# An attention and gated-MLP kernel in fp32r: operands of its matmuls at another distance modulo 256 bytes

## The chip, the cores and the metric

The kernel runs on one core of one Trainium2 chip. The metric is the device time of the program in microseconds. Before the change it is 687.74 us in the median of three runs (687.03 to 688.06). The engines are named as in the profile: PE is TensorE's matmul, PEld its weight load, DVE VectorE, ACT ScalarE, POOL GpSimd, and SPq the queue from which SyncE issues transfers. A matmul has a stationary operand, which a weight load puts into the array, and a moving operand, which streams through it.

## The reference

All inputs are fp32. There are 8 batches, 12 heads, 448 positions, a head dimension of 64, a model width of 768 and a hidden width of 1024 (two halves of 512).

```python
# attention with a sigmoid in place of the softmax
scores = scale * np.matmul(q, k.transpose(0, 1, 3, 2)) - np.log(S)
attn = 1.0 / (1.0 + np.exp(-scores))
x = np.matmul(attn, v)                     # heads side by side: (8, 448, 768)
# gated MLP with a spatial product
h = np.maximum(x @ w_in, 0.0)
u, v = h[..., :512], h[..., 512:]
v_n = (v - mean(v)) / np.sqrt(var(v) + 1e-6)
v_s = np.einsum('ts,bsd->btd', w_spatial, v_n) + b_spatial[None, :, None]
out = (u * v_s) @ w_out
```

## The kernel before

Most products are made in the number type fp32r, to which an fp32 value is split as a high and a low part: a cast gives the high part, a subtraction the low one. A product of two split operands is three matmuls, in the order of `TERMS` (line 224): high times high, low stationary times high moving, high stationary times low moving. Each matmul loads its stationary operand of 128 columns anew. Tiles of split operands hold both parts one behind the other in the same partition.

The work goes over four pairs of batches (`m`). Within a pair these stages follow on TensorE, and the names are those of the profile:

- Scores `psc` (line 249): for a pair of heads that lies in the two halves of the partitions, 128 keys are stationary and 448 queries moving. Two matmuls of 64 rows each run beside each other, one per head. Keys and queries lie in one tile, `qks`: 384 keys at its start, the queries from column `REST` = 384 on. The last 64 keys of two heads are multiplied in plain fp32 from the loaded tile `raw` (line 237).
- `pav` (line 279): attention times values in plain fp32; stationary the values `v`, moving the sigmoids `at`. Its result is split into `x_s`, which holds 12 heads of two batches.
- `pv` (line 290, as all below): the v half of the hidden layer, 128 positions of `x_s` stationary, 512 columns of `w_in` moving.
- `pg`: the spatial product, normalised values `vn` stationary, `w_sp_s` moving with 448 columns.
- `pu`: the u half, `w_in` stationary and `x_s` moving with 448 columns.
- `po`: the output, `w_out_s` stationary and the gated values `gs` moving with 448 columns.

The order is written out by hand: `attention`, the loop at the end of the program, and `in_program_order`, which keeps each engine to the order in which the program names its work. Transfers are all issued from SyncE's queue, several heads ahead (`start_loads`, `ahead`). VectorE and ScalarE split the loaded keys and queries (`attention_splits`), empty the accumulators and split the results.

SBUF positions follow from the pools. The pool `small` comes first; an unused tile `fill` of 152 columns stands at its end (line 95). Then come the constants in the order of lines 97 to 101, then the buffers of `work`, each kind (`raw`, `v`, `tmp`, `big`, `split`, `wval`) with as many buffers as it asks for. In the built program of before, each of these tiles starts in its partition at a multiple of 256 bytes, and so does each slice of them that a matmul reads.

Of the kernel before, what the change touches and what calls it, by code (L numbers as in the profile page):

```python
# [8 lines left out]
F32 = mybir.dt.float32  # L9
F32R = mybir.dt.float32r  # L10
# [4 lines left out]
P = 128  # L15
# [20 lines left out]
def attn_gmlp_kernel(  # L36
# [25 lines left out]
    nc = tc.nc  # L62
    B, NHP, _, _ = qk.shape
    S = out.shape[3]
    D = P // 2
    NCC = out.shape[1]
    DM = NCC * P
    F = w_in.shape[1] // (4 * NCC)
    NFC = F // P
    HALF = 64  # L70
    NFULL = 3

    REST = NFULL * P
    PART = REST + S
    QK = 1.0 / math.sqrt(D)
    NEG_LOG_S = -math.log(S)
# [2 lines left out]
    small = ctx.enter_context(tc.tile_pool(name="small", bufs=2))  # L79
    const = ctx.enter_context(tc.tile_pool(name="const", bufs=1))  # L80
    work = ctx.enter_context(tc.tile_pool(name="work", bufs=2))
# [10 lines left out]
    table = small.tile([P, 1], F32, name="table", bufs=1)  # L92
    nc.scalar.activation(table, bias_s, AF.Sigmoid)

    small.tile([P, 152], F32, name="fill", bufs=1)

    w_in_s = const.tile([P, 2 * NCC, 2, F], F32R, name="w_in_s")
    w_out_s = const.tile([P, NFC * DM // 512, 2, 512], F32R, name="w_out_s")
    w_sp_s = const.tile([P, 4, 2, 512], F32R, name="w_sp_s")
    b_bc = const.tile([P, 512], F32, name="b_bc")  # L100
    x_s = const.tile([P, 2, NCC, 2 * S], F32R, name="x_s")

    def split(hi, lo, src, copy):
        copy(hi, src)  # L104
        nc.vector.tensor_sub(lo, src, hi.bitcast(F32))  # L105
# [30 lines left out]
    def weight_steps():  # L136

        steps = []
        for i in range(NCC):
            steps += [(w_in, w_in_s, NCC + i)] + [(w_sp, w_sp_s, i)] * (i < NFC)  # L140
        steps += [(w_in, w_in_s, i) for i in range(NCC)]
        steps += [(w_out, w_out_s, i) for i in range(NFC * DM // 512)]
        raws = {}

        def load(n):
            if n < len(steps):
                src, _, i = steps[n]
                w = 512 if src is w_sp else 1024

                if n < NFIRST:  # L150
                    raw = work.tile([P, 1024], U32, tag="tmp", name=f"wraw_{n}", bufs=3)[:, :w]
                else:
                    raw = work.tile([P, 1024], U32, tag="raw", name=f"wraw_{n}", bufs=4)
                raws[n] = raw.bitcast(F32) if src is w_sp else raw
                nc.sync.dma_start(raws[n], src[:, i * w : (i + 1) * w])

        for n in range(AHEAD):
            load(n)
        yield
        for n, (src, dst, i) in enumerate(steps):  # L160
            load(n + AHEAD)
            if src is w_sp and i == 0:
                nc.sync.dma_start(b_bc, b_sp.broadcast_to([P, 512]))
            hi, lo = dst[:, i, 0], dst[:, i, 1]
            val = raws.pop(n)
            if src is not w_sp:
                raw = val
                val = work.tile([P, 512], U32, tag="wval", name=f"wval_{n}", bufs=1)
                yield from convert(val, raw)
                val = val.bitcast(F32)  # L170
            split(hi, lo, val, nc.vector.tensor_copy)
            yield


    NFIRST = NCC + NFC + 3
    BLOCK = 3

    weights = weight_steps()

    def load_weights(n):  # L180
# [4 lines left out]
    values = {}  # L185

    def attention_loads(b, hp):
        raw = work.tile([P, 1024], F32, tag="raw", name=f"raw_{b}_{hp}", bufs=4)[:, : 2 * S]
        cut = REST - P if b == hp == 0 else 0
        nc.sync.dma_start(raw[:, cut:], qk[b, hp, :, cut:])  # L190
        if cut:
            nc.sync.dma_start(raw[:, :cut], qk[b, hp, :, :cut])
        loaded[b, hp] = raw
# [13 lines left out]

    def attention_splits(b, hp):
        raw = loaded[b, hp]
        s = work.tile([P, 2, PART], F32R, tag="split", name=f"qks_{b}_{hp}", bufs=3)  # L210
        if b == hp == 0:

            chunk, rest, query = slice(REST - P, REST), slice(0, REST - P), slice(REST, PART)
            nc.vector.tensor_copy(s[:, 0, chunk], raw[:, chunk])
            for cols in (query, rest):
                nc.scalar.copy(s[:, 0, cols], raw[:, cols])
            for cols in (chunk, query, rest):
                nc.vector.tensor_sub(s[:, 1, cols], raw[:, cols], s[:, 0, cols].bitcast(F32))
        else:
            scalar = b == 1 or b == 0 and hp not in (1, 2)  # L220
            split(s[:, 0], s[:, 1], raw[:, :PART], nc.scalar.copy if scalar else nc.vector.tensor_copy)
        parts_of[b, hp] = s

    TERMS = ((0, 0), (1, 0), (0, 1))
# [4 lines left out]
    def attention_scores(b, hp, t):  # L229
# [3 lines left out]
        if t == NFULL:  # L233
            for odd in range(2):
                raw = loaded[b, hp + odd]
                for j, rows in enumerate(heads):
                    nc.tensor.matmul(  # L237
                        psc[odd * HALF : (odd + 1) * HALF, j, :S],
                        raw[rows, PART : PART + HALF],
                        raw[rows, REST:PART],  # L240
                        start=True,
                        stop=True,
                    )
        else:
            s = parts_of[b, hp + t // (NFULL + 1)]
            k = (t % (NFULL + 1) + NFULL - 1) % NFULL * P
            for i, (a, e) in enumerate(TERMS):
                for j, rows in enumerate(heads):
                    nc.tensor.matmul(  # L249
                        psc[:, j, :S],  # L250
                        s[rows, a, k : k + P],
                        s[rows, e, REST:PART],
                        start=i == 0,
# [40 lines left out]
    def gate_values(m, ts):  # L294

        n = len(ts)
        pv = banks(f"pv_{m}_{ts[0]}")
        for i, t in enumerate(ts):
            product(
                pv[:, i, :F],  # L300
                [
                    (
                        lambda a, cc=cc, t=t: x_s[:, a, cc, t * P : (t + 1) * P],
                        lambda c, cc=cc: w_in_s[:, NCC + cc, c, :],
                    )
                    for cc in range(NCC)
                ],
            )
        rv = work.tile([P, 2, 512], F32, tag="tmp", name=f"rv_{m}_{ts[0]}", bufs=3)
        nc.scalar.activation(rv[:, :n], pv[:, :n], AF.Relu)  # L310
        mv = small.tile([P, 2, 2], F32, tag="mv", name=f"mv_{m}_{ts[0]}")
        for i in range(n):
            stats = small.tile([P, 6], F32, tag="stats", name=f"stats_{m}_{ts[i]}")
            nc.vector.bn_stats(stats, rv[:, i])  # L314
            nc.vector.bn_aggr(mv[:, i], stats)
        rstd = small.tile([P, 2], F32, tag="rstd", name=f"rstd_{m}_{ts[0]}")
        nc.gpsimd.tensor_scalar_add(rstd[:, :n], mv[:, :n, 1], 1e-6)
        nc.gpsimd.tensor_tensor(rstd[:, :n], rstd[:, :n], mhalf[:, :n], op=ALU.pow)
        for i in range(n):
            nc.vector.tensor_scalar_sub(rv[:, i], rv[:, i], mv[:, i, 0:1])  # L320
        for i, t in enumerate(ts):
            vn = work.tile([P, 2, 512], F32R, tag="big", name=f"vn_{m}_{t}", bufs=7)
            if t != NFULL:
                parts = [(vn[:, 0], vn[:, 1], slice(0, P))]
            else:

                a, c = slice(0, HALF), slice(HALF, P)
                parts = [(vn[a, 0], vn[c, 0], a), (vn[c, 1], vn[a, 1], c)]
            for hi, lo, rows in parts:
                nc.vector.tensor_scalar_mul(hi, rv[rows, i], rstd[rows, i : i + 1])  # L330
                nc.vector.scalar_tensor_tensor(
                    lo,
                    rv[rows, i],
                    rstd[rows, i : i + 1],
                    hi.bitcast(F32),
                    op0=ALU.mult,
                    op1=ALU.subtract,
                )
            vns[t] = vn
# [33 lines left out]
    def gated(b, fcs):  # L373

        odd = b % 2
        g = gates.pop((b, fcs))
        pu = banks(f"pu_{b}_{fcs[0]}")
        for i, fc in enumerate(fcs):
            fs = slice(fc * P, (fc + 1) * P)
            product(  # L380
                pu[:, i, :S],
                [
                    (
                        lambda a, cc=cc: w_in_s[:, cc, a, fs],
                        lambda c, cc=cc: x_s[:, c, cc, odd * S : (odd + 1) * S],
                    )
                    for cc in range(NCC)
                ],
            )
        nc.vector.scalar_tensor_tensor(g, pu[:, :, :S], 0.0, g, op0=ALU.max, op1=ALU.mult)  # L390
        products[b, fcs] = g
# [13 lines left out]
    def output(b, es, part=None):  # L405
# [9 lines left out]
        po = sums_of[es]  # L415
        n = NFC // 2
        for i, e in enumerate(es):

            def weight(a, fc, e=e):
# [6 lines left out]
                    (lambda a, fc=fc: weight(a, fc), lambda c, fc=fc: hidden[b, fc][:, c])  # L426
                    for fc in (range(NFC) if part is None else range(part * n, (part + 1) * n))
                ],
# [70 lines left out]
    load_weights(1)  # L499

    zeros = work.tile([P, 512], F32R, tag="big", name="zeros", bufs=7)
    nc.vector.memset(zeros.bitcast(F32), 0.0)  # L502
    idle = banks("idle")
    for _ in range(6):
# [98 lines left out]
```

## Time and profile before

| what | value |
|---|---|
| median of three runs | 687.74 us (687.03 to 688.06) |
| the profiled execution | 687.04 us |
| its span, first to last instruction | 685.3 us |
| matmuls and weight loads | 3838 each |
| mean granted clock of TensorE | 0.999 |

The span is the time from the first to the last instruction of one execution that the hardware profiler recorded; 1.7 us of that execution lie outside it. A row of a group gives its line, engine, operation, result and operands, shapes and count, then the busy time in us and the mean duration of one in ns, then the idle time of its engine before it and what ended that. A row of the chain gives its start and length in us, the engine, the result, the line and the count. A row of a tile's view gives the count, the least, median and greatest duration in ns, and the first and last start in us.

Plain fp32 matmuls appear in the trace as two instructions each. Matmuls overlap, since a matmul's record ends when its last result is out, and the next stream begins earlier.

### The profile page before, as it was taken

The numbers are of one execution on the slowest core, as the hardware profiler recorded it, in microseconds if no ns is written. First come the engines' busy times: TensorE is split into PE (matmuls) and PEld (weight loads), VectorE is DVE, ScalarE is ACT, GpSimd is POOL, SyncE is SP. The second block draws the span as 40 slices with busy tenths as digits, with TensorE's granted clock in tenths as the row PEclk, the third lists the DMA queues.
The fourth block names the chain that finished last, engine by engine and source line by source line (L and its number), as shares of the span: only waits on it lengthen the run. The fifth ranks groups of instructions, "written<-read, shape, count | busy, mean of one in ns | idle before, by whom it ended". The sixth has DMA issues, their size and how long they took to land.

```text
span 685.3 us, 9090 instructions
## 1 busy us (share of the span) xinstructions
PE 679.9 (99%) x3838; PEld 504.2 (74%) x3838; DVE 293.6 (43%) x471; ACT 240.9 (35%) x285; POOL 18.5 (3%) x36
## 2 busy tenths in 40 slices
PE   9999999999999999999999999999999999999997
PEld 5454889998554488999854458899984455889997
DVE  6999888803244237221233514721224241562111
ACT  7886110112577510011367651011137774101111
POOL 0000010000000001000000001100000000110000
PEclk9999999999999999999999999999999999999999
DMA  8872202230534000003062400000315310000102
GB/s 324 299 258 85 87 5 85 88 129 27 174 123 162 28 1 0 1 28 107 28 205 96 158 28 0 1 1 27 108 55 188 120 43 1 0 1 0 55 28 80
DMA packets 20552, 55.37 MB, mean 81 GB/s; under 512 B 1952, under 2 KB 8352, under 8 KB 20512
## 3 DMA queue, kind: packets, MB, share of 16 engines
q1 hardware_dynamic: 20512, 54.80, 23.4%
q8 instruction: 30, 0.49, 0.3%
q14 instruction: 10, 0.08, 0.0%
HBM read 43.78 MB, written 11.01 MB: 80 GB/s over the span
## 4 chain that ended last, share of the span: by engine, by line
PE 99%; DVE 0%; issue 0%; ACT 0%; ACTq 0%
PE pav L279 20%; PE po L290 17%; PE pu L290 17%; PE pv L290 17%; PE psc L249 15%; PE pg L290 10%; PE psc L237 3%; PE idle L505 0%; ACT osb L437 0%; DVE zeros L502 0%; DVE bias_s L88 0%; DVE mhalf L90 0%; ACTq L437 0%
## 5 line engine op out<-in xcount | busy, mean ns | idle before, releaser
L257 ACT ACTIVATE at<-psc,bias_s 128x896 f32<-128x896 f32 x168 | 158.5, 1008 | 60.0 <-PE psc L249 57.6
L279 PE MATMUL pav<-at,v 128*64 128x448 f32 (+1 forms) x768 | 139.4, 546 | 0.0
L290 PE MATMUL po<-gs,w_out_s 128*128 128x448 f32 x576 | 118.6, 366 | 0.0
L290 PE MATMUL pu<-x_s,w_in_s 128*128 128x448 f32 x576 | 118.0, 365 | 0.0
L290 PE MATMUL pv<-w_in_s,x_s 128*128 128x512 f32 x504 | 115.4, 390 | 0.0
L290 PEld LDWEIGHTS po<-gs,w_out_s 128*128 128x128 f32 x576 | 107.9, 188 | 9.7 <-ACT at L257 0.9
L290 PEld LDWEIGHTS pu<-x_s,w_in_s 128*128 128x128 f32 x576 | 108.2, 188 | 8.6
L290 PEld LDWEIGHTS pv<-w_in_s,x_s 128*128 128x128 f32 x504 | 94.3, 188 | 22.3 <-issue 2.8
L249 PEld LDWEIGHTS psc<-qks 64*128 64x128 f32 x864 | 76.8, 185 | 39.3 <-ACT at L257 15.5
L279 PEld LDWEIGHTS pav<-at,v 128*64 128x64 f32 (+1 forms) x768 | 44.0, 135 | 82.2 <-issue 76.5
L249 PE MATMUL psc<-qks 64*128 64x448 f32 x864 | 102.6, 377 | 0.2
L105 DVE TENSOR_TENSOR x_s<-pav,x_s 128x448 fp32r<-128x448 f32 x48 | 29.6, 623 | 125.6 <-ACT x_s L104 125.6
L290 PE MATMUL pg<-w_sp_s,vn 128*128 128x448 f32 x352 | 72.7, 365 | 0.0
L290 PEld LDWEIGHTS pg<-w_sp_s,vn 128*128 128x128 f32 x352 | 66.1, 188 | 5.4
L390 DVE SCALAR_TENSOR_TENSOR g<-pu,g 128x896 f32<-128x896 f32 x16 | 17.4, 1090 | 121.3 <-PE pu L290 121.3
L441 ACT COPY osb<-po 128x896 f32<-128x896 f32 x23 | 20.9, 907 | 118.4 <-PE po L290 110.2
L104 ACT CAST gs<-g 128x896 fp32r<-128x896 f32 x16 | 15.1, 941 | 129.9 <-DVE g L390 129.9
L310 ACT ACTIVATE rv<-pv 128x1024 f32<-128x1024 f32 (+1 forms) x16 | 14.8, 922 | 100.8 <-PE pv L290 100.8
L105 DVE TENSOR_TENSOR qks<-raw,qks 128x832 fp32r<-128x832 f32 x47 | 48.2, 1025 | 1.8 <-ACT qks L104 0.5
L104 DVE CAST qks<-raw 128x832 fp32r<-128x832 f32 x38 | 22.3, 586 | 32.6 <-PE po L290 31.1
L104 ACT CAST x_s<-pav 128x448 fp32r<-128x448 f32 x48 | 25.5, 532 | 28.7 <-PE pav L279 28.7
L314 DVE BATCH_NORM_STATS2 stats<-rv 128x6 f32<-128x512 f32 x28 | 19.0, 679 | 38.5 <-ACT rv L310 38.5
(38 smaller groups left out, 229.8 us busy)
## 6 DMA issues: line engine op xcount, KB each, us to landing
raw<-qk_dram SPq DMA_DIRECT2D x47, 448.0 KB, 4.3
v<-v_dram SPq DMA_DIRECT2D x23, 448.0 KB, 4.5
out_dram<-osb SPq DMA_DIRECT2D x23, 448.0 KB, 2.6
wraw<-w_in_dram SPq DMA_DIRECT2D x12, 512.0 KB, 4.1
wraw<-w_out_dram SPq DMA_DIRECT2D x6, 512.0 KB, 3.7
wraw<-w_sp_dram SPq DMA_DIRECT2D x4, 256.0 KB, 5.3
out_dram<-osb SPq DMA_DIRECT2D x2, 224.0 KB, 2.1
raw<-qk_dram SPq DMA_DIRECT2D x1, 320.0 KB, 2.9
```

The source lines that it names most:

```text
L104: copy(hi, src)
L105: nc.vector.tensor_sub(lo, src, hi.bitcast(F32))
L237: nc.tensor.matmul(psc[odd * HALF : (odd + 1) * HALF, j, :S], raw[rows, PART : PART + HALF], raw[rows, REST:PART], start=True, stop=True,)
L249: nc.tensor.matmul(psc[:, j, :S], s[rows, a, k : k + P], s[rows, e, REST:PART], start=i == 0, stop=i == len(TERMS) - 1,)
L257: nc.scalar.activation(at, psc[:, :, :S], AF.Sigmoid, bias=bias_s, scale=QK)
L279: nc.tensor.matmul(pav[heads, :S], vt[rows, t, heads], at[rows, j], start=start, stop=stop)
L290: nc.tensor.matmul(ps, st, mv, start=start and i == 0, stop=stop and i == len(ops) - 1)
L310: nc.scalar.activation(rv[:, :n], pv[:, :n], AF.Relu)
L314: nc.vector.bn_stats(stats, rv[:, i])
L390: nc.vector.scalar_tensor_tensor(g, pu[:, :, :S], 0.0, g, op0=ALU.max, op1=ALU.mult)
L441: nc.scalar.copy(osb, whole_of.pop(es)[:, :, :S])
```

## The change

The change moves tiles in SBUF and leaves what is computed as it is. It has four parts:

- `w_in_s` becomes two tiles, `w_v_s` and `w_u_s`. The tensor `w_in` is cut into the same two halves, and the list of loads names them in the same order as before.
- The constants are declared in another order: `w_sp_s`, `x_s`, `w_v_s`, an unused tile `fill_u` of 192 bytes, `w_u_s`, `w_out_s`, `b_bc`. The tile `fill` shrinks from 152 to 24 columns. An unused tile `fill_split` of 64 bytes is put into `work` ahead of `split`.
- Keys and queries lie 16 columns (64 bytes) further apart: `REST` is 400 where it was 384. The host puts 16 zeros between them, each head pair's load has 912 columns where it had 896, and its split 848 where it had 832.
- The buffers for `qks` are declared with the 896 columns per part that `gs`, which shares them, had already.

In the built program this gives the following positions, in bytes modulo 256; before, all are 0.

| matmuls | count | stationary after | moving after | stationary minus moving after |
|---|---|---|---|---|
| `psc`, line 249 (keys, queries) | 864 | 0 | 64 | 192 |
| `pg` (`vn`, `w_sp_s`) | 352 | 192 | 0 | 192 |
| `pu` (`w_u_s`, `x_s`) | 576 | 192 | 0 | 192 |
| `po` (`w_out_s`, `gs`) | 576 | 192 | 0 | 192 |
| `pv` (`x_s`, `w_v_s`) | 504 | 0 | 0 | 0 |
| `pav` (`v`, `at`) | 768 | 192 | 192 | 0 |
| `psc`, line 237 (short keys, queries in `raw`) | 192 | 0 | 0 | 0 |

```diff
+    w_u, w_v = (w_in[:, j * 2 * NCC * F : (j + 1) * 2 * NCC * F] for j in range(2))
...
-    REST = NFULL * P
+    FULL = NFULL * P
+    GAP = 16
+    REST = FULL + GAP
     PART = REST + S
...
-    small.tile([P, 152], F32, name="fill", bufs=1)
-
-    w_in_s = const.tile([P, 2 * NCC, 2, F], F32R, name="w_in_s")
+    small.tile([P, 24], F32, name="fill", bufs=1)
+
+    w_sp_s = const.tile([P, 4, 2, 512], F32R, name="w_sp_s")
+    x_s = const.tile([P, 2, NCC, 2 * S], F32R, name="x_s")
+    w_v_s = const.tile([P, NCC, 2, F], F32R, name="w_v_s")
+    const.tile([P, 48], F32, name="fill_u")
+    w_u_s = const.tile([P, NCC, 2, F], F32R, name="w_u_s")
     w_out_s = const.tile([P, NFC * DM // 512, 2, 512], F32R, name="w_out_s")
-    w_sp_s = const.tile([P, 4, 2, 512], F32R, name="w_sp_s")
     b_bc = const.tile([P, 512], F32, name="b_bc")
-    x_s = const.tile([P, 2, NCC, 2 * S], F32R, name="x_s")
...
-        raw = work.tile([P, 1024], F32, tag="raw", name=f"raw_{b}_{hp}", bufs=4)[:, : 2 * S]
-        cut = REST - P if b == hp == 0 else 0
+        raw = work.tile([P, 1024], F32, tag="raw", name=f"raw_{b}_{hp}", bufs=4)[:, : 2 * S + GAP]
+        cut = FULL - P if b == hp == 0 else 0
...
-        s = work.tile([P, 2, PART], F32R, tag="split", name=f"qks_{b}_{hp}", bufs=3)
+        s = work.tile([P, 2, 2 * S], F32R, tag="split", name=f"qks_{b}_{hp}", bufs=3)
...
-            split(s[:, 0], s[:, 1], raw[:, :PART], nc.scalar.copy if scalar else nc.vector.tensor_copy)
+            split(s[:, 0, :PART], s[:, 1, :PART], raw[:, :PART], nc.scalar.copy if scalar else nc.vector.tensor_copy)
...
-                        lambda c, cc=cc: w_in_s[:, NCC + cc, c, :],
+                        lambda c, cc=cc: w_v_s[:, cc, c, :],
...
-                        lambda a, cc=cc: w_in_s[:, cc, a, fs],
+                        lambda a, cc=cc: w_u_s[:, cc, a, fs],
...
     zeros = work.tile([P, 512], F32R, tag="big", name="zeros", bufs=7)
+    work.tile([P, 16], F32, tag="fill_split", name="fill_split", bufs=1)
...
-    qk = np.concatenate([full[:, :, P:], full[:, :, :P], q, short], axis=2)
+    gap = np.zeros((B, H, 16, D), q.dtype)
+    qk = np.concatenate([full[:, :, P:], full[:, :, :P], gap, q, short], axis=2)
```

More of the change, by code (lines that the diff above doesn't have):

```diff
@@ L139, in weight_steps @@
         for i in range(NCC):
-            steps += [(w_in, w_in_s, NCC + i)] + [(w_sp, w_sp_s, i)] * (i < NFC)
-        steps += [(w_in, w_in_s, i) for i in range(NCC)]
+            steps += [(w_v, w_v_s, i)] + [(w_sp, w_sp_s, i)] * (i < NFC)
+        steps += [(w_u, w_u_s, i) for i in range(NCC)]
         steps += [(w_out, w_out_s, i) for i in range(NFC * DM // 512)]
@@ L209, in attention_splits @@
         raw = loaded[b, hp]
-        s = work.tile([P, 2, PART], F32R, tag="split", name=f"qks_{b}_{hp}", bufs=3)
+        s = work.tile([P, 2, 2 * S], F32R, tag="split", name=f"qks_{b}_{hp}", bufs=3)
         if b == hp == 0:
-            chunk, rest, query = slice(REST - P, REST), slice(0, REST - P), slice(REST, PART)
+            chunk, rest, query = slice(FULL - P, FULL), slice(0, FULL - P), slice(REST, PART)
             nc.vector.tensor_copy(s[:, 0, chunk], raw[:, chunk])
@@ L568 @@
     full, short = k[:, :, :H0], k[:, :, H0:]
-    qk = np.concatenate([full[:, :, P:], full[:, :, :P], q, short], axis=2)
-    qk = np.ascontiguousarray(np.transpose(qk, (0, 1, 3, 2))).reshape(B, H // 2, 2 * D, 2 * S)
+    gap = np.zeros((B, H, 16, D), q.dtype)
+    qk = np.concatenate([full[:, :, P:], full[:, :, :P], gap, q, short], axis=2)
+    qk = np.ascontiguousarray(np.transpose(qk, (0, 1, 3, 2))).reshape(B, H // 2, 2 * D, 2 * S + 16)
     vT = np.transpose(v.reshape(B, H // 4, 2, 2, S, D), (0, 1, 4, 2, 3, 5)).reshape(B, H // 4, S, 2, 2 * D)
```

## The prediction

> **What bounds the kernel now.** I read the page first: the engines' shares, the granted clock, and the chain that ended last.
>
> ```profile
> span 685.3 us, 9090 instructions
> ...
> PE 679.9 (99%) x3838; PEld 504.2 (74%) x3838; DVE 293.6 (43%) x471; ACT 240.9 (35%) x285; POOL 18.5 (3%) x36
> ...
> PEclk9999999999999999999999999999999999999999
> ...
> PE 99%; DVE 0%; issue 0%; ACT 0%; ACTq 0%
> PE pav L279 20%; PE po L290 17%; PE pu L290 17%; PE pv L290 17%; PE psc L249 15%; PE pg L290 10%; PE psc L237 3%; PE idle L505 0%; ACT osb L437 0%; DVE zeros L502 0%; DVE bias_s L88 0%; DVE mhalf L90 0%; ACTq L437 0%
> ```
>
> TensorE is busy for 99% of the span, the chain is TensorE for 99%, and the clock is granted in full throughout. So no wait can be taken away; what moves the time is how far apart the matmuls start. The busy rows by group don't tell that, since matmuls overlap: one `pu` lasts 365 ns, but the next begins long before. The pieces of the chain do tell it, because a piece of n matmuls in a row that takes t has a spacing of t/n.
>
> ```profile
> 68.81 28.78 PE pv L290 x126
> 97.59 8.92 PE pg L290 x44
> 106.51 14.59 PE pu L290 x72
> ...
> 130.02 14.59 PE po L290 x72
> ...
> 188.39 2.04 PE psc L249 x18
> ```
>
> `pu`, `po` and `pg` all stream 448 columns: 14.59/72 = 202.6 ns, 202.6 ns and 8.92/44 = 202.7 ns apart. `pv` streams 512 columns: 28.78/126 = 228.4 ns. The scores `psc` run in pairs, one head in each half of the rows, so 18 of them are nine pairs, 227 ns a pair with the entry after another kind of matmul counted in.
>
> Per column the 512-wide product takes 228.4/512 = 0.446 ns and the 448-wide one 202.6/448 = 0.452 ns. At `pv`'s rate 448 columns would take 199.9 ns. So each 448-wide product has 2.7 ns that the wider one has not, although a cost fixed per product would weigh on both alike in ns. The spread of the durations points to the same place:
>
> ```profile
> L290 PEld LDWEIGHTS pu<-x_s,w_in_s x576: 187/188/188, 106.1 to 666.6; 128*128 128x128 f32 x192
> L290 PE MATMUL pu<-x_s,w_in_s x576: 362/365/369, 106.3 to 666.8; 128*128 128x448 f32 x192
> ...
> L290 PE MATMUL pv<-w_in_s,x_s x504: 389/389/499, 68.7 to 605.1; 128*128 128x512 f32 x168
> ...
> L290 PE MATMUL pg<-w_sp_s,vn x352: 362/365/370, 97.4 to 637.6; 128*128 128x448 f32 x176
> ...
> L249 PEld LDWEIGHTS psc<-qks x864: 182/184/334, 4.4 to 570.4; 64*128 64x128 f32 x173
> L249 PE MATMUL psc<-qks x864: 355/362/739, 4.4 to 570.6; 64*128 64x448 f32 x173
> ```
>
> The three numbers are the least, the median and the greatest duration. `pv` lies at 389 from its least to its median, while `pu` and `pg`, whose work is the same every time, go from 362 to 369 or 370. The weight load of 187 to 188 ns is the same in all. Something makes the 448-wide streams uneven by a few ns, with a weight load running beside each of them (PEld is busy 74% of the span). A clash of two reads, of the next stationary operand and of the stream under way, is one thing that could do this, and the distance of their addresses is what the change alters.
>
> **The change part by part.** The order of instructions on all five engines stays the same, one for one; no instruction is added or removed.
>
> *Addresses.* Before, every operand of a matmul starts at a multiple of 256 bytes. After, the stationary operand is 192 past the moving one, modulo 256, in `pu` (576), `po` (576), `pg` (352) and the scores of line 249 (864 matmuls, 432 pairs): 1936 places in the row of TensorE. In `pv`, `pav` and the 64-key scores the difference stays 0. The trace of before holds no matmul with another difference than 0, so the price is bounded from both sides. At the favourable end, the next weight load starts only when a product starts, so a spacing can't fall below the load of 188 ns: 202.6 - 188 = 14.6 ns less, times 1936 = 28.3 us. At the other end stands the worst duration that these streams now show, 370 against 365: 5 ns more, 9.7 us. I see no reason that excludes either sign. Between them I take the row that is nearest in kind: the same engine, load and number type, without the unevenness, `pv`. That is 2.7 ns less per place, and the least durations (362 against 365, 3 ns) say about the same. So 1504 x 2.7 = 4.1 us from `pu`, `po` and `pg`, and 432 x 2.7 = 1.2 us from the scores; of these the scores are the less certain, since their entries hide the steady spacing.
>
> *A rule against it.* The Trainium skill, "TensorE: Matmul & The Clock Gate" (Step-by-step, LDWEIGHTS), says that TensorE reads SBUF through two independent ports, so that loading the next weights takes no bandwidth from the running matmul. By that rule this term is nothing and the time stays; it is the first rival below. The same page's formula for spacing, N/2.4 + 2.5 ns, would give 189.2 ns for 448 columns against the 202.6 measured, so the page leaves 13 ns of each product unexplained, and a sum by it, were they all to go, would be about 26 us.
>
> *The gap between keys and queries.* It widens 47 splits from 832 to 848 columns, and the loads by the same 16 columns.
>
> ```profile
> L105 DVE TENSOR_TENSOR qks<-raw,qks 128x832 fp32r<-128x832 f32 x47 | 48.2, 1025 | 1.8 <-ACT qks L104 0.5
> L104 DVE CAST qks<-raw 128x832 fp32r<-128x832 f32 x38 | 22.3, 586 | 32.6 <-PE po L290 31.1
> ...
> raw<-qk_dram SPq DMA_DIRECT2D x47, 448.0 KB, 4.3
> ```
>
> 16/832 of the two VectorE rows (48.2 and 22.3 us) is 1.4 us, and ScalarE's nine casts of 885 ns add 0.2 us. The cover is TensorE's own stream: VectorE is idle for 57% of the span. In the first stage, where VectorE is busiest, the cover is thinnest; if all of that were exposed, it would cost 1.6 us. A load grows from 448 to 456 KB, 1.8% of 4.3 us or 0.08 us, and it is issued far ahead, except the first, which TensorE awaits: 656 columns instead of 640, some 0.07 us of its 2.9 us. I take 0.1 us for the whole.
>
> ```profile
> L104 ACT CAST qks<-raw 128x832 fp32r<-128x832 f32 x9 | 8.0, 885 | 0.0
> ...
> raw<-qk_dram SPq DMA_DIRECT2D x1, 320.0 KB, 2.9
> ```
>
> *`w_in` in two tiles, the order of the tiles, the fills.* The same loads into the same number of bytes, no instruction: 0. No other work hides this; there is nothing to hide.
>
> Sum: -4.1 - 1.2 + 0.1 = -5.2 us. The profiled execution took 687.04 us with a span of 685.3, so 1.7 us lie around the span and don't change: 687.04 - 5.2 = 681.8. The median of the three runs, 687.74, is 0.7 above the profiled one; on its level the forecast is 682.5 us.
>
> **The rivals.**
>
> *Nothing happens.* The two reads don't meet, and the uneven beat comes from elsewhere (the accumulation, the issue). For it: the load's duration is the same 187 to 188 ns beside 448 and 512 columns, as if nothing disturbed it, and `pu`, `po` and `pg` have one spacing although their operands lie in different tiles. Against it: a beat in work that never varies wants a cause, and two streams that run beside each other are at hand. The time would be 687.04 + 0.1 on the profiled level, 687.8 on the median's. This is also what the skill's rule above gives.
>
> *It opens the whole gap.* If nearly all that a 448-wide product takes above its weight load is a clash, which 192 bytes avoid, the spacing falls towards 188 ns: 14.6 x 1936 = 28 us, 659 us; half of it, 673 us. For it: nothing on the page accounts for the distance from 188 to 202.6. Against it: `pv` with its smooth beat pays per column almost the same, which suggests that most of this is the stream itself.
>
> *The new distance clashes more.* The stationary read is slower per byte than the stream: 128 columns in 188 ns against 448 in 202.6. So the stream runs through the addresses modulo 256 several times while one load runs, and overtakes it at some moment whatever the distance; 192 bytes choose only the moment. If it falls where the stream has just settled, each product takes the place of today's worst, 369 or 370 against 365: 4 ns more on 1936 places, 7.7 us, 695.5 us on the median's level. It decides as soon as the spacing of `pu` exceeds 203.4 ns (0.7 ns x 1936 = 1.4 us). For it: today's common distance 0 lets some products through at 362, so it is not the worst. Against it: today some pay 369.
>
> **How the numbers follow.** The forecast gets 0.43; the whole gap, or a good part of it, 0.13; nothing 0.22; more clashes 0.22. A difference under 0.2% (1.4 us) can hardly be told from none here. So faster 0.56, same 0.22, slower 0.22. The likeliest case by itself reaches from 679.5 to 685.5 us (1.2 to 4.3 ns per place). For 8 in 10 the range must take in no change, half of the slower case and half of the larger gain: 667 to 693 us, which leaves out about 0.09 at each end.
>
> **What would show it.** If right, the chain's pieces of `pu` and `po` with 72 matmuls fall from 14.59 to about 14.40 us and `pg` with 44 from 8.92 to 8.80, the durations' spread narrows, and `pv` with 126 stays at 28.8, since its distance is unchanged. If nothing happens, all stay within 0.02 us. If the whole gap opens, `pu` takes 13.5 to 14.0 us. If clashes grow, `pu` takes 14.7 us or more, and its median duration is near 369. If `pu` gains and the scores don't, the gain is 4 us and not 5. A change of `pv` or `pav` would show that a cause outside the operands' distance is at work. The forecast would be wrong altogether if TensorE began to wait at the splits, which would appear as idle time before `psc`.

## The result, and the profile after

The changed kernel takes 682.87 us in the median of four runs (682.57 to 683.52), the kernel before 687.62 us beside it (687.03 to 688.06). The ratio is 0.9932 with a 95% interval of 0.9916 to 0.9948, so 4.75 us are gone. The profiled execution took 683.03 us, with a span of 681.2 against 685.3.

The chain of the changed kernel, in the same stage as the rows of the prediction (start and length in us, result, line, count):

```profile
69.14 28.79 PE pv L295 x126
97.94 8.80 PE pg L295 x44
106.73 14.40 PE pu L295 x72
...
129.94 14.40 PE po L295 x72
```

`pu` and `po` fell from 14.59 to 14.40, `pg` from 8.92 to 8.80, and `pv`, whose distance did not change, stayed. The starts in the trace give the steady spacing: 202.7 ns before and 200.0 after for all three. The single spacings are not equal: they repeat in a short series, which is called the beat below. Before, five of them repeated (203, 199, 207, 202, 203), after, three (201, 201, 198). The views of the tiles show shorter durations (least, median, greatest). The median fell from 365 to 362 ns for `pu` and `pg`; of these two, only `pg` got a narrower spread:

```profile
L295 PE MATMUL pu<-x_s,w_u_s x576: 360/362/368, 106.6 to 662.9; 128*128 128x448 f32 x192
...
L295 PE MATMUL pg<-w_sp_s,vn x352: 360/362/363, 97.8 to 634.1; 128*128 128x448 f32 x176
...
L254 PE MATMUL psc<-qks x864: 357/360/739, 4.4 to 567.6; 64*128 64x448 f32 x173
```

One piece of the kernel before stands out. Three times a `po` follows scores of the next pair of batches, and these three had the same work and the same distance 0. The first took 15.06 us, the other two 14.79:

```profile
161.26 15.06 PE po L290 x72
...
330.76 14.79 PE po L290 x72
```

By its starts the first holds no longer wait; it has another beat: it settles at 206.7 ns, the others at 202.7. After the change all three take 14.61 us, at 200.0 ns.

The scores' median duration fell too, from 362 to 360, but the runs of nine pairs hardly got shorter, and the pieces of the short-key scores behind them got longer. The chain before, for one pair of heads:

```profile
203.38 2.02 PE psc L249 x18
205.40 0.93 PE psc L237 x8
```

and after:

```profile
202.42 2.01 PE psc L254 x18
204.43 0.95 PE psc L242 x8
```

The short-key scores' weight load waits for ScalarE's sigmoid, before and after (us in total, times, longest):

```profile
PEld psc L237 <- ACT at L257: 7.0, 21, 0.4
```

```profile
PEld psc L242 <- ACT at L262: 7.2, 21, 0.4
```

So the 4.1 us of span divide thus: 1504 x 2.67 ns = 4.0 us in `pu`, `po` and `pg`; some 0.06 us in each attention stage behind the first; 0.27 us in the one `po` that before had the slower beat; and 0.37 us that the first scores took longer. The last two differ between executions of the same work. TensorE speeds up during the first stage's scores: in these two profiles their pairs start first 540 and then some 373 ns apart, and later about 200. The wide spacings were two before and four with the change, and the piece of these nine pairs took 2.43 and 2.80 us; in the experiments' profiles it took from 2.16 to 3.54:

```profile
4.42 2.80 PE psc L254 x16
```

```profile
4.42 2.16 PE psc L254 x17
```

```profile
4.42 3.54 PE psc L255 x14
```

(The first is the changed kernel, the second the changed kernel with the finer map behind it, the third the last experiment below.) The wider splits cost VectorE 1.1 us, off the path:

```profile
L110 DVE TENSOR_TENSOR qks<-raw,qks 128x848 fp32r<-128x848 f32 x47 | 49.0, 1042 | 1.8 <-ACT qks L109 0.5
L109 DVE CAST qks<-raw 128x848 fp32r<-128x848 f32 x38 | 22.6, 596 | 32.1 <-PE po L295 30.3
```

### The profile page after: what moved, and what is told of

The parts are those of the page before. It is cut to its first block, busy times and chain, and to the rows that moved or that the text cites. A ratio compares the mean times of both kernels' runs of the same rounds, so it can differ in the third digit from the quotient of the medians.

```text
span 681.2 us, 9090 instructions
## 1 busy us (share of the span) xinstructions
PE 675.9 (99%) x3838; PEld 504.1 (74%) x3838; DVE 294.8 (43%) x471; ACT 241.0 (35%) x285; POOL 18.5 (3%) x36
## 4 chain that ended last, share of the span: by engine, by line
PE 99%; DVE 0%; ACT 0%; issue 0%; ACTq 0%
PE pav L284 20%; PE po L295 17%; PE pu L295 17%; PE pv L295 17%; PE psc L254 15%; PE pg L295 10%; PE psc L242 3%; PE idle L511 0%; ACT osb L442 0%; DVE zeros L508 0%; DVE bias_s L91 0%; DVE mhalf L93 0%; ACTq L442 0%
## 5 line engine op out<-in xcount | busy, mean ns | idle before, releaser
L295 PE MATMUL po<-gs,w_out_s 128*128 128x448 f32 x576 | 116.9, 362 | 0.0
L295 PE MATMUL pu<-x_s,w_u_s 128*128 128x448 f32 x576 | 116.5, 362 | 0.0
L295 PE MATMUL pv<-w_v_s,x_s 128*128 128x512 f32 x504 | 115.4, 390 | 0.0
L295 PEld LDWEIGHTS pu<-x_s,w_u_s 128*128 128x128 f32 x576 | 108.0, 187 | 7.2
L295 PEld LDWEIGHTS pv<-w_v_s,x_s 128*128 128x128 f32 x504 | 94.3, 188 | 22.3 <-issue 2.8
L110 DVE TENSOR_TENSOR qks<-raw,qks 128x848 fp32r<-128x848 f32 x47 | 49.0, 1042 | 1.8 <-ACT qks L109 0.5
L109 DVE CAST qks<-raw 128x848 fp32r<-128x848 f32 x38 | 22.6, 596 | 32.1 <-PE po L295 30.3
```

What stands on the lines that cost most here:

```text
L295: nc.tensor.matmul(ps, st, mv, start=start and i == 0, stop=stop and i == len(ops) - 1)
```

## The experiments

The theory to be tested was that the distance between the stationary and the moving operand, modulo 256 bytes, sets the spacing. The rivals were that the position of an operand by itself does it, or the new layout in some other way.

### All tiles moved, distances kept

```diff
 # the kernel before
-    small.tile([P, 152], F32, name="fill", bufs=1)
+    small.tile([P, 200], F32, name="fill", bufs=1)
```

> The kernel before with all its tiles 192 bytes further on: every operand starts at 192 past a multiple of 256, and every distance between a stationary and a moving operand stays 0. Theory 'distance' (the two reads of a matmul meet according to the difference of their addresses): pieces of 72 pu stay at 14.59 us, the time at 687.6. Rival 'position' (a stationary operand that starts at 192 is read better, wherever the moving one lies): 14.40 us and about 683 us, as in the changed kernel.

It took 687.79 us against 687.60 for the kernel before, ratio 1.0004 (0.9994 to 1.0014), and its pieces of 72 `pu` and 44 `pg` are those of before:

```profile
97.40 8.92 PE pg L290 x44
106.31 14.59 PE pu L290 x72
```

Position alone does nothing that can be measured. Again one of the three `po` behind the scores took 15.06 us, but here it was the second and not the first.

### A map of distances, 448 columns

Rows of matmuls were put behind the last output of the changed kernel, each row a source line of its own, so that the chain shows one piece per row. The same was done in the next runs.

```diff
+    probe = banks("probe")
+    for _ in range(40): nc.tensor.matmul(probe[:128, 0, :448], w_v_s[:, 0, 0, 0:128], x_s[:, 0, 0, 0:448], start=True, stop=True)
+    for _ in range(40): nc.tensor.matmul(probe[:128, 0, :448], w_v_s[:, 0, 0, 4:132], x_s[:, 0, 0, 0:448], start=True, stop=True)
...
```

> The changed kernel, with 25 rows of 40 matmuls more at its end (448 columns in each, their result is not used), one source line per row; the time grows by about 200 us and is not compared. Rows 1 to 16: stationary operand at 0, 16, ... 240 bytes, moving at 0. Theory 'distance': row 1 (0) has a spacing of 202.6 ns, row 13 (192) of 200.0, the others lie between 198 and 207 and not all alike. Rows 17 to 21 (moving at 64, 128, 192 with stationary at 0; both at 64; both at 192): by 'distance' 200.0 (distance 192), then as rows 9 and 5, then 202.6 twice; by 'position' 202.6 three times, then as row 5, then 200.0. Rival 'layout' (the gain came from other tiles or the cut of w_in): all 21 rows alike. Rows 22 to 25 load only 64 and 32 columns, at distance 0 and 192: if the unevenness is a clash with the load, the spacing falls clearly below 200 ns with a shorter load, by about half and three quarters of what is above the bare stream; if it comes from the stream alone, it stays at 202.6.

The chain's pieces, here for the distances 0, 64, 96, 192 and 224, then for distance 192 by moving the moving operand to 64, then for both operands at 64 (distance 0):

```profile
677.46 8.26 PE probe L557 x40
...
710.25 8.09 PE probe L561 x40
...
726.47 8.01 PE probe L563 x40
...
775.23 8.00 PE probe L569 x40
...
791.41 8.26 PE probe L571 x40
...
807.79 8.02 PE probe L573 x40
...
832.05 8.25 PE probe L576 x40
```

8.00/40 is 200 ns, 8.26/40 is 206.5. The spacing follows the distance and not the position, and since the rows are not all alike, the new layout by itself does not set it. The expected 202.6 at distance 0 did not come: the row settled at 206.7, the beat that one `po` of the kernel before had shown. Loads of 64 and 32 columns did not bring the spacing below 200 ns either (202.2 and 202.2 at distance 0, 201.1 and 206.6 at distance 192). With the moving operand at 128 and 192 the rows took 204.0 and 202.3, as distances 128 and 64 do.

### The same for 512 columns and for pairs

> The changed kernel with 26 rows of 40 matmuls at its end (result not used). Rows 1 to 16 stream 512 columns with the stationary operand at 0, 16, ... 240 and the moving at 0. Theory 'distance', with a fixed price per load: row 1 at 226.7 ns as pv, and at 192 also about 226.7 or 2.6 less; 'distance matters only where the length leaves an uneven beat': all 16 within 1 ns of 226.7. Rows 17 to 26: 256, 320, 384, 416, 480 columns, each at distance 0 and 192. A bare stream would fall in proportion to the columns (about 0.42 ns a column); where the load becomes the bound the spacing stops falling, near 190 ns, from 416 or 384 columns down, and the distance makes no difference there.

> The changed kernel with 16 rows of 40 pairs at its end, each pair as in the scores: two matmuls of 64 rows and 448 columns beside each other, stationary at 0, 16, ... 240 bytes, moving at 0 (result not used). Theory 'distance, in the scores too': the pairs are spaced as the full matmuls, 202.6 ns at 0 and 200.0 at 192, so that the scores' term of the forecast was lost in the short runs of nine pairs or in waits. Rival 'the halves do not clash': all 16 rows alike, and the scores could gain nothing.

All three maps, in ns, from the starts of the last 30 matmuls or pairs of each row:

| distance | 448 columns | 448, pairs | 512 columns |
|---|---|---|---|
| 0 | 206.7 | 202.7 | 226.7 |
| 16 | 206.7 | 206.7 | 226.7 |
| 32 | 204.4 | 204.4 | 233.3 |
| 48 | 202.2 | 202.2 | 233.3 |
| 64 | 202.2 | 202.2 | 233.3 |
| 80 | 203.3 | 203.3 | 232.0 |
| 96 | 200.0 | 200.0 | 234.3 |
| 112 | 204.0 | 204.0 | 233.3 |
| 128 | 204.0 | 204.0 | 233.3 |
| 144 | 202.2 | 202.2 | 233.4 |
| 160 | 205.3 | 205.3 | 233.3 |
| 176 | 203.4 | 203.4 | 230.2 |
| 192 | 200.0 | 200.0 | 228.9 |
| 208 | 204.4 | 204.4 | 231.9 |
| 224 | 206.6 | 206.7 | 233.4 |
| 240 | 203.3 | 203.3 | 228.4 |

For 512 columns distance 0 is the best and 192 is 2.2 ns worse: both halves of the expectation on 192 failed. Pairs behave as full matmuls and could gain 2.7 ns a pair in a long run.

The rows with other lengths show what lies beneath. The chain's pieces for 512 columns (distance 16), for 320 (distance 0) and for 384 (distance 192):

```profile
687.00 9.07 PE probe L558 x40
...
835.48 5.87 PE probe L575 x40
...
854.17 6.94 PE probe L578 x40
```

By the starts that is 226.7, 146.7 and 173.3 ns. The line through these values is 0.417 ns a column and 13.3 ns fixed. It gives 200.0 for 448 columns, which is the best of the whole map, and the worse distances of this map lie up to 7 ns above it. At 384 columns both distances, 0 and 192, are on the line (173.3); at 320 too. Not every length reaches it: 416 columns took 188.3 ns at both distances, where the line gives 186.7, and 480 took 216.7 and 218.3, where it gives 213.3. Nor is it a floor everywhere: 256 columns took 120.0 at distance 0, on the line, but 113.3 at 192. The bound by the weight load that the expectation named does not exist, since these 256 columns run 113 to 120 ns apart with loads of 188 ns, which overlap. That the distance makes no difference at the short lengths failed with them too.

### The map's other best and one of its worst, in the kernel

```diff
 # far224: distance 224        # d96: distance 96
-    const.tile([P, 48], F32, name="fill_u")
+    const.tile([P, 56], F32, name="fill_u")      # d96: [P, 24]
...
-    work.tile([P, 16], F32, tag="fill_split", name="fill_split", bufs=1)
+    work.tile([P, 8], F32, tag="fill_split", name="fill_split", bufs=1)      # d96: [P, 40]
```

> The changed kernel, with pu, pg and po at distance 224 in place of 192 (one unused tile is 32 bytes longer, another 32 shorter); the scores keep 192, pv and pav 0. Theory 'distance': the row at 224 of the map had 206.6 ns against 200.0 at 192, so 6.6 ns x 1504 = 9.9 us more than the changed kernel: about 692.8 us, 5 us above the kernel before; pieces of 72 pu at 14.88 us. Rival 'the map's beat doesn't carry over' (in the kernel high and low parts alternate; at distance 0 the map had 206.7 and the kernel 202.6): anything from 682.9 to 692, with 72 pu below 14.75.

> The changed kernel, with pu, pg and po at distance 96, the other row of the map that had 200.0 ns. Theory 'distance': 72 pu in 14.40 us and the time of the changed kernel, 682.9 within 0.5. Rival 'the map's beat doesn't carry over': 72 pu between 14.5 and 14.9, 684 to 690 us.

Distance 224 took 692.4 us, ratio 1.0069 (1.0053 to 1.0084), as expected. Distance 96 took 692.8 us, ratio 1.0074 (1.006 to 1.0087), 10 us more than expected. Both have 14.88 us for 72 `pu` and 9.09 for 44 `pg`, 206.7 ns a product. The chain at distance 96:

```profile
98.42 9.09 PE pg L295 x44
107.51 14.88 PE pu L295 x72
```

The durations sit at the top of what the kernel before showed (distance 224):

```profile
L295 PE MATMUL pu<-x_s,w_u_s x576: 367/369/369, 106.9 to 671.9; 128*128 128x448 f32 x192
```

So the rival of the prediction in which the new distance is worse is real. And the theory, that the distance alone sets the spacing, had fallen: 96 gives 200.0 in the map and 206.7 in the kernel.

Not every piece of these two kernels runs at 206.7 ns. Of the three `po` behind the scores, distance 224 had 15.06, 14.61 and 15.06 us, distance 96 had 14.61, 15.06 and 14.61. Two of them, the second of each kernel (distance 224, then 96):

```profile
333.52 14.61 PE po L295 x72
```

```profile
333.47 15.06 PE po L295 x72
```

By the starts these are steady at 200.0 and 206.7 ns. So both distances have a fast and a slow beat, and the same code in one execution takes now the one, now the other. The entry goes with it: in all such `po` at distances 0, 224 and 96 the first spacing was 306 or 307 ns where the slow beat followed and 310 where the fast one did.

### The changed kernel without the gap in the scores

```diff
-    GAP = 16
+    GAP = 0
...
-    gap = np.zeros((B, H, 16, D), q.dtype)
+    gap = np.zeros((B, H, 0, D), q.dtype)
```

(and the load's 16 columns less)

> The changed kernel without the gap between keys and queries: the scores of line 249 are at distance 0 again, loads have 896 columns and splits 832, all else stays. By the forecast's term of 1.2 us for the scores it would take 684.1 us. Theory 'the runs of nine pairs give it back' (2.02 us before and 2.01 after for such a run, and a later wait for ScalarE that grows by as much): 682.9, within 0.3; the pieces of 18 psc at 2.02 and those of 20 pav unchanged at 3.16.

It took 682.97 us (682.67 to 683.57), ratio 0.9931 (0.9919 to 0.9943): the same as the changed kernel. The scores' part of the change is worth nothing that can be measured in the time. Its chain has 2.02 or 2.01 us for nine pairs and 0.93 for the short keys, as the kernel before. By the starts, the first pair of a run of nine takes some 310 ns with either distance, and the last, where `pav` follows, some 295. The seven spacings between them fell with the change from 202.6 to 200.5 ns on average. Runs that lead to `pav` got 19 ns shorter by it; runs that lead to the short-key scores got 10 ns longer, since the wait for ScalarE's sigmoid there grew. In all, an attention stage behind the first takes 0.065 us less than before with the gap and 0.052 us less without it.

### A finer map, and what ran before

> The changed kernel with 55 rows of 32 matmuls at its end (448 columns, moving at 0, result not used). 48 rows have the stationary operand at every multiple of 4 bytes below 256 that is not one of 16; if reads go by units of 16 bytes, the rows within one unit are alike or change smoothly; if some distance beats 200.0 ns by a ns or more, a better kernel is to be had (1.5 us per ns). Three rows at 256, 352 and 448 bytes: by a period of 256 they repeat 0, 96 and 192 (206.7 or 202.6, 200.0, 200.0); by a longer period they don't. The last four rows: 512 columns at 0, then 448 at 0, 448 at 192, 448 at 0. If distance 0 has two steady beats (202.6 in the kernel, 206.7 in the map), which one it takes depends on what ran before it: 202.6 after the row of 512 columns, as in the kernel after pv, and 206.7 after the row at 192, as in the map.

No distance is below 200.0, but several others reach it (8, 20, 36, 108, 200, 248, 252), and two are worse than any of the first map (148 with 207.8 and 212 with 209.1). Neighbours have nothing in common: 4 bytes 204.5, 8 bytes 200.0, 12 bytes 203.3, so no unit of 16 bytes shows in it. Each row was entered from the row before it, though, and as the next rows show the entry counts too, so these maps do not give the distance alone. 352 and 448 repeat 96 and 192 with 200.0; 256 took 202.7, which is the other beat of distance 0. The last four rows of the chain:

```profile
1009.09 7.30 PE probe L608 x32
1016.39 6.48 PE probe L609 x32
1022.87 6.40 PE probe L610 x32
1029.27 6.48 PE probe L611 x32
```

Distance 0 settles at 202.7 behind the 512-wide row, as in the kernel behind `pv`. Behind the row at 192 it settled at 202.7 too, not at the 206.7 of the first map, where the row also came behind products at 192, the kernel's last `po`. So the distance of what ran before does not decide by itself.

To test the entry by itself, rows were entered from a 512-wide row, and 96 also from a row at 192. Loads of other widths and steps, other lengths and bf16 were added.

> The changed kernel with more rows at its end (result not used). First block: rows of 448 columns at distances 96, 224, 192, 64, 16 and 0, each entered from a row of 512 columns at 0, as pg is entered from pv. Theory 'entry': the steady beat depends on the distance and on what ran before; entered so, 96 gives 206.7 (200.0 in the map) and 192 still 200.0. Rival 'high and low parts': 96 gives 200.0 here too, since the row uses one pair of operands, and the kernel's 206.7 comes from the change of operands. Then 448 at 96 entered from 192: 200.0 by 'entry'. Loads of 64 and 32 columns at distances 0 and 192, entered from the 512-wide row, and loads of 128 columns that are 8 bytes apart: if each byte of the load that is read takes time from the stream, the spacing above the bare stream falls with the width and grows with the step; if only the moment of the load counts, they lie between 200 and 207 without such an order. 384 and 256 columns at six distances: 173.3 and 113.3 or 120.0 as before, or a spread of up to 7 ns as with 448. bf16, 448 and 512 columns: with half the bytes per column, all distances alike, at 0.417 ns a column and a fixed part of 13 ns or less.

The chain's pieces: a 512-wide row, then 96; a 512-wide row, then 192; and later 192, then 96.

```profile
677.25 5.49 PE probe L557 x24
682.74 8.25 PE probe L558 x40
...
704.70 5.48 PE probe L561 x24
710.18 8.00 PE probe L562 x40
...
759.07 4.81 PE probe L569 x24
763.88 8.01 PE probe L570 x40
```

The same operands at the same distance 96 run at 206.7 ns when entered from 512 columns and at 200.0 when entered from 192. High and low parts have no share in it, since one pair of operands was used. With loads of 128 columns, 192 settles at 200.0 from every entry that was tried.

Loads again show no order by width or step: entered from 512 columns, distance 0 took 202.2 with 64 and with 32 columns, distance 192 took 201.2 and 206.7, and loads with columns 8 bytes apart took 203.3 at both. 384 columns spread from 173.3 to 176.8 over six distances, 256 from 113.3 to 120.0. In bf16 the four distances that were tried are alike once the rows have settled:

```profile
895.72 4.56 PE probe L598 x24
900.27 4.54 PE probe L599 x24
904.81 4.54 PE probe L600 x24
909.35 4.54 PE probe L601 x24
```

4.54/24 is 189.2 ns for 448 columns at 64, 96 and 192, the first row having 11 ns at its entry; 512 columns took 215.8 at 0 and 192. These agree with the formula N/2.4 + 2.5 ns in the Trainium skill, "TensorE: Matmul & The Clock Gate" (Back-to-back issue gap), which gives 189.2 and 215.8. The section means it for isolated matmuls and gives about 131 ns for a stream with loads at 512 columns, which these rows, with a load for each matmul, do not bear out. For fp32r the runs say 10.8 ns more at best. The rule of the Trainium skill, "TensorE: Matmul & The Clock Gate" (Step-by-step, LDWEIGHTS), that a weight load takes nothing from the running matmul, fits the bf16 rows; for fp32r the spacing does depend on where the two operands lie. The loads differ as well: they last 97 ns in bf16 and 188 in fp32r.

### The entry, in the kernel

If the entry decides, a kernel with distance 96 must become fast when only the products between `pv` and `pu` lie at 192.

```diff
 # d96, with the spatial weights at 160, so that pg has distance 192; pu and po keep 96
-    small.tile([P, 24], F32, name="fill", bufs=1)
+    small.tile([P, 64], F32, name="fill", bufs=1)
...
     w_sp_s = const.tile([P, 4, 2, 512], F32R, name="w_sp_s")
+    const.tile([P, 24], F32, name="fill_x")
```

> The kernel with pu and po at distance 96, but pg, which comes between pv and pu, at distance 192. Theory 'entry': pg takes its 200.0 from pv's beat, and pu, entered from there, now stays at 200.0 at distance 96: pieces of 44 pg 8.80, 72 pu 14.40, time 682.9. Rival 'distance 96 is bad in the kernel, whatever runs before': pg 8.80, pu and po 14.88, about 690.5 us.

It took 683.55 us, ratio 0.9936 (0.992 to 0.9953). `pu` and `po` at distance 96, which cost 206.7 ns where `pg` had 96 too, now run at 200.1:

```profile
98.68 8.80 PE pg L296 x44
107.48 14.41 PE pu L296 x72
121.90 8.81 PE pg L296 x44
130.71 14.42 PE po L296 x72
```

Of the 9 us between the two kernels, 352 x 6.6 ns = 2.3 us are `pg`'s own, whose distance changed. The rest lies in `pu` and `po`, whose operands stayed where they were modulo 256 bytes: it comes from the beat that `pg` hands on. No version beat the changed kernel: its three products are at the lowest spacing that any of the distances gave, and `pv` is at its own lowest.

## Why the prediction was right, and where it was not

**The bound.** That only the spacing of matmuls could move the time was right. No other piece of the chain moved by more than 0.4 us.

**The main term.** 2.7 ns on 1504 products, 4.1 us, against 2.67 ns and 4.0 us measured. The pieces came out as written: 14.40, 8.80, and `pv` at 28.8. That the durations' spread narrows came true for `pg` only.

But the step from which the 2.7 ns came was wrong. It took `pv`'s price per column, 0.446 ns, for what an undisturbed product pays, and set aside a price per product. The maps show the contrary: 0.417 ns a column and a fixed 13.3 ns. `pv`'s 228.4 ns also held its entries, while its steady spacing is 226.7. With that, the step would have said 226.7 x 448/512 = 198.3 and a gain of 4.3 ns. The two errors cancelled, and that the size was right is luck. The least duration, 362 against 365, is no better witness: the changed kernel's `pu` again has 360 against 362, and no distance gave less than its 200.0 ns. The prediction also took distance 0 to have one spacing, and passed over the piece of 15.06 us, in which the kernel before shows the second.

**The scores' term.** 1.2 us was forecast and next to nothing came, as the kernel without the gap shows. The step that failed is "432 pairs at the same 2.7 ns". In a long run pairs do gain 2.7 ns. In a run of nine the seven middle spacings gained 2.1 ns, the first and the last none, and about half of what was gained went into the longer wait for ScalarE's sigmoid. The prediction had named the scores as the less certain part, and a gain of 4 us without them.

**The loads and splits.** 0.1 us forecast, none seen on the chain. VectorE works 1.1 us longer under TensorE's stream.

**The sum.** 682.5 forecast, 682.87 measured; without the scores' term, and with 0.1 us for the loads as it stands, the working gives a gain of 4.0 us and 683.7. The profiled executions differ by 4.0 us, and the interval of the measured gain, 3.6 to 5.8 us, holds it. Where the other 0.8 us of the medians lies is not shown. The pieces that change between executions are large enough for it: the first scores, and up to 0.27 us in each `po` behind the scores, which has two beats at distance 0 and had one in every profile at 192. That the sum came within 0.4 us is luck in part, since the scores' term in it did not come.

**The rivals.** "Nothing happens" fell. "It opens the whole gap" fell: 200.0 is the least of 64 distances, and the weight load is no floor. "The new distance clashes more" did not happen at 192, but is true of 224 and of 96: they cost 4.0 ns more than before on most products, as that rival priced it. The whole came to 4.7 and 5.1 us instead of its 7.7: the scores stayed at 192, which leaves 1504 x 4.0 = 6.0 us, and in the profiles one or two of the `po` behind the scores ran at 200.0, which takes off about 0.5 us each. Its argument, that the stream overtakes the load at some moment, is not shown.

**The cause.** The prediction named a clash between the read of the next stationary operand and the stream. Shown is that the distance matters, that position and layout do not, that several steady beats can exist at one distance, and that the entry has a part in choosing among them. The period of 256 bytes rests on six rows that fit it: three with the moving operand shifted, and those at 256, 352 and 448. Not shown is the clash itself. A shorter load does not bring the spacing below 200.0, a load with twice the step does not drive it up in order, and neighbours 4 bytes apart differ by 4 ns. That bf16, with half the bytes per column, did not depend on the distance fits a limit in reading, but does not prove it, since its loads are shorter too. What in the chip makes the beat, and what in an entry selects it, stays open.

## What to carry to other kernels

When TensorE is the bound, divide the chain's pieces by their counts and look at the single spacings: the position of the operands may give time back, here 2.7 of 202.7 ns. An uneven beat by itself does not say that there is some: the changed kernel beats too (201, 201, 198), at the lowest spacing that was found. The best distance is not one number. It depends on the length of the stream (192 for 448 columns, 0 for 512) and on what ran before, so try it in the kernel itself, where a row measured alone may settle on another beat, and prefer a distance that settles well from every entry. The runs of nine pairs here gained next to nothing from it.

## What the runs showed that was not expected

- One distance can have two steady beats: 0 ran at 202.7 or 206.7, 96 and 224 at 200.0 or 206.7. In the `po` behind the scores even the same code in one execution took now one, now the other.
- A product can hand its beat on: `pg` at 192 in place of 96 made `pu` and `po` 6.6 ns faster per product, though nothing of theirs had changed.
- At the best distances, a matmul in fp32r with a load for each product has a fixed price of 13.3 ns above 0.417 ns a column at 320, 384, 448 and 512 columns; in bf16 it is 2.5 ns at 448 and 512.
- Weight loads of 188 ns do not keep matmuls of 256 columns from running 113 ns apart.
- The first scores, during which TensorE speeds up (pairs 373 ns apart, then 200), took from 2.16 to 3.54 us in different executions, a difference of 0.2% of the whole.
